# Copies of odd heads' v and the scaling of turned k moved from ScalarE to GpSimd, with a new list of the order of work

## The chip, the cores and the metric

The kernel runs on one core of a Trainium2 chip. The metric is the device time of one execution in microseconds, the median of several runs: 478.81 us for the kernel before (three runs, 478.62 to 479.23). One more execution was recorded by the profiler.

The engines are named as in the profile: PE is TensorE, ACT ScalarE, DVE VectorE, POOL GpSimd, SP SyncE, which here only issues DMAs.

## The reference

An attention block with a decaying state is followed by a feed-forward block of products. For each of 4 batches and 8 heads, over 768 steps t with head size 48:

```python
cur   = einsum('d,e->de', u * k[t], v[t])
y[t]  = einsum('d,de->e', r[t], state + cur)
state = w[:, None] * state + einsum('d,e->de', k[t], v[t])
```

y, laid out as 3,072 tokens of 384 numbers, goes through

```python
out = ((x @ w1) * (x @ w2)) @ w3 @ w_out
```

with w1 and w2 of 384 x 1024, w3 of 1024 x 1024 and w_out of 1024 x 384. The weights arrive as 64-bit numbers.

## The kernel before

**Tiling.** The sequence is cut into 6 chunks of 128 steps; a unit is one chunk of one batch, so there are 24 units, n = 4c + b. For each unit k and r are multiplied by powers of w (scale, L453), turned so that the head size lies on the partitions (on PE for units 0 to 4, turn_k L500; through DRAM for later ones), and k times r gives a masked 64 x 64 block for each half chunk and head. That block times v, plus r times the running state, is y. The term with u is made in two ways: for units 0 to 4 (EARLY, L447) the turned k is scaled by a column of u (put_u, L597, word ku) and multiplied with r on PE (own_products, L603, word Au), then laid on the diagonal of the masked block (own_mask, L607, word mo); for later units DVE multiplies k, r and u (L462, L465, L469) and ACT multiplies the sums with v (L483).

The products with odd heads read v from the other half of the partitions, so odd_values (L709, word vs) copies the odd heads' v of each unit crosswise, two copies of 64 x 192 per unit into one of three buffers. with_pairs (L725, word V) reads it.

**Weights.** Each weight comes in 32 pieces through three buffers (fetch, L266, word W; the first eight are strips of w1 and w2, the next eight are w_out, the last sixteen w3). A piece is converted in five words: M on ACT, N and H on DVE, L on ACT, Q on DVE; L frees the buffer. Then w3 and w_out are folded into one 1024 x 384 matrix: for each of eight blocks DVE turns a block of w3 (word G, L434), PE multiplies it with w_out (word F, L439), ACT takes it (word X, L442). From then on a chunk needs two products with w1 and w2 (words a and b, or in halves pa and pb with sums ga and gb) and one with the folded matrix (words P, each eight matmuls of 128 x 192, L829, with sums E, L845 to L859, and stores D, L863). The rows of the result are gathered in two buffers (`bufs=2`) taken in turn by the upper and lower rows of each pair.

**Order.** ORDER is a list of 1,417 words written out by hand or by a planner. A word names a step, its unit or piece, and the PSUM banks it takes. Each engine runs its instructions in the order of the list, and starts one when the semaphores of what it needs are there:

```python
with tc.manual_schedule(engines={PE, ACT, DVE, SP}):
    for word in ORDER.split():
        word, _, at = word.partition("/")
        chosen_banks[:] = map(int, at)
        name, *at = word.split(".")
        names[name](*map(int, at))
```

Of the words that the prediction speaks of, T, R, A, Au, S, U, V, yt, F and P are PE's; t, r, M, L, ku, vs, X and yx are ACT's; k, N, H, Q, i, j (state), m and mo (masks), fe, d, e, f, u, G and most of E are DVE's; v, kr, W, y, z and D are issued by SP. Z is a filler of matmuls whose result is not used (busy_array, L953). x, y, z and l turn k and r of later units through DRAM.

Of the kernel before, what the change touches and what calls it, by code (L numbers as in the profile page):

```python
# [27 lines left out]
fe.1/0 k.3 Au.2 V.1/10 L.2 W.4 i.2/4 R.3/2 m.2 kr.5 Y.1/10 T.3/4 r.3/2 k.4 yt.1/1 t.3/4 W.5 mo.2 ku.3 R.4/0 j.2/5  # L28
S.2/24 A.3 yx.1/1 Q.1 Au.3 yx.0/3 T.4/5 r.4/0 v.4 Q.2 a.0.0.0/1 M.3 N.3 vs.2 m.3 a.0.1.0/3 t.4/5 H.3 c.0.0.0/1 vs.3
N.4 U.3/05 L.3 fe.2/4 mo.3 V.2/24 c.0.1.0/3 i.3/0 M.4 k.5 A.4 v.5 Y.2/24 S.3/13 W.6 b.0.1.0/0 H.4 ku.4 fe.3/3 Q.3 L.4  # L30
yt.2/2 V.3/13 u.0.1.0/0 d.5 W.7 Au.4 Y.3/13 ub N.5 U.4/40 M.5 kr.6 yt.3/1 b.0.0.0/3 H.5 yx.3/1 yx.2/2 vs.4 Q.4
a.0.2.2/1 L.5 cz.1 N.6 vs.5 W.8 j.3/5 Q.5 a.0.0.1/2 kr.7 u.0.0.0/3 M.7 N.7 a.0.1.1/5 c.0.2.2/1 H.7 x.5 a.0.5.2/3 L.7
# [5 lines left out]
c.0.7.2/4 W.18 Q.15 M.17 N.17 Q.14 z.6 H.17 b.0.7.2/5 u.0.3.2/1 L.17 Q.17 W.20 G.0 b.0.6.2/4 M.18 cz.0 v.7 N.18 M.19
N.19 H.18 H.19 L.18 F.0/1 x.7 c.0.4.2/3 W.21 L.19 Q.18 Q.19 M.20 W.22 N.20 vs.6 e.6 H.20 G.1 L.20 W.23 f.6 M.21 F.1/3
Q.20 N.21 y.7 H.21 u.0.6.2/4 L.21 M.22 Q.21 W.24 G.2 N.22 H.22 F.2/4 j.5 L.22 N.23 M.23 W.25 u.0.4.2/0 yx.4/2 H.23  # L40
Q.22 L.23 l.6 Q.23 W.26 N.24 M.24 G.3 X.1/3 z.7 S.5/02 U.6 fe.5/2 H.24 M.25 A.6 d.7 V.5/02 L.24 kr.8 N.25 F.3/3 H.25
Q.24 L.25 Y.5/02 M.26 W.28 Q.25 N.26 H.26 G.4 L.26 W.29 m.6 F.4/0 X.3/3 i.6 l.7 W.27 u.0.7.2/5 X.0/1 j.6 X.2/4 M.28
# [5 lines left out]
f.9 xs.1.0 pa.1.1.0/1 xs.1.1 s.0.0.0 pa.1.0.4/5 xs.1.2 wa.3 pa.1.0.5/3 E.0.1.1/0 d.10 pa.1.0.1/2 i.9 ga.1.0.1/3 vs.10
wb.0 xs.1.3 yt.8/0 ga.1.0.3/45 pa.1.0.6/3 yx.8/0 k.10 pb.1.0.0/0 ga.1.0.2/3 wb.2 ga.1.0.5/2 pa.1.0.3/3 m.9 vs.9 e.10
x.10 pb.1.0.4/2 ga.1.0.7/3 k.11 y.10 gb.1.0.0/30 pa.1.0.7/5 j.9 pa.1.0.2/4 wb.1 wb.3 z.10 ga.1.0.4/5 pb.1.0.5/3 B.0  # L50
pb.1.0.1/0 gb.1.0.1/3 kr.13 ga.1.0.6/4 gb.1.0.3/42 pb.1.0.6/3 kr.12 gb.1.0.5/0 f.10 pb.1.0.7/2 gb.1.0.2/3 pb.1.0.3/3
pb.1.0.2/4 gb.1.0.7/3 gb.1.0.4/2 ga.1.1.0/31 g.9 d.11 pa.1.1.5/3 B.1 kr.14 pa.1.1.1/1 B.3 ga.1.1.1/3 l.10 x.11
# [1033 lines left out]
```

## Time and profile before

| | us |
|---|---|
| median of three runs | 478.81 |
| lowest and highest | 478.62, 479.23 |
| the profiled execution | 479.13 |
| its span | 477.0 |

| engine | busy us | share of the span |
|---|---|---|
| PE | 463.4 | 97% |
| DVE | 324.3 | 68% |
| ACT | 199.4 | 42% |
| POOL | 4.4 | 1% |

The span runs from the first instruction to the last event of the profiled execution; the 2.1 us between it and the execution's time lie around it. A matmul's end is modelled, so PE's busy share is a share of time in which it had work, not of its peak. In the rows below, an instruction's "idle before" is the time its engine stood still before it, followed by what released it.

### The profile page before, as it was taken

How to read it: one execution, taken by the hardware profiler on the slowest of the kernel's cores; microseconds unless marked ns; L12 is line 12 of the kernel's file. 1: busy time of each engine (PE TensorE's matmuls, PEld its weight loads, DVE VectorE, ACT ScalarE, POOL GpSimd, SP SyncE). 2: the span in 40 equal slices, each digit the busy share in tenths (PEclk: the TensorE clock that was granted, in tenths of full speed). 3: DMA queues.
4: the chain of work that ended last, by engine and by line, in shares of the span. 5: the costliest groups of instructions: out<-in, count | busy, mean ns of one | idle time of the engine just before them, and what ended most of it. 6: DMA issues, size and time to landing. Idle time of an engine off the chain costs nothing. (4 is left out here: it accounts for less than half of the span.)

```text
span 477.0 us, 12147 instructions
## 1 busy us (share of the span) xinstructions
PE 463.4 (97%) x5072; PEld 391.3 (82%) x5072; DVE 324.3 (68%) x668; ACT 199.4 (42%) x464; POOL 4.4 (1%) x17
## 2 busy tenths in 40 slices
...
GB/s 180 234 283 240 205 225 211 225 218 200 155 68 118 122 114 110 141 68 166 116 133 105 52 99 118 48 53 85 1 84 1 19 16 26 8 18 0 35 36 88
DMA packets 100481, 52.74 MB, mean 111 GB/s; under 512 B 79296, under 2 KB 89792, under 8 KB 100416
## 3 DMA queue, kind: packets, MB, share of 16 engines
...
q14 instruction: 23, 0.19, 0.1%
q10 hardware_dynamic: 624, 0.00, 0.1%
...
## 5 line engine op out<-in xcount | busy, mean ns | idle before, releaser
L917 PE MATMUL ps_accB<-x,w 128*128 128x256 f32 x160 | 45.1, 384 | 0.0
L439 PE MATMUL ps_w<-wo,w3T 128*128 128x384 f32 x128 | 42.5, 488 | 0.5 <-DVE w3T L434 0.3
L483 ACT ACTIVATE ynat<-vnat,dg 128x48 f32<-128x48 f32 x144 | 34.3, 323 | 17.8 <-DVE dg L469 14.7
L439 PEld LDWEIGHTS ps_w<-wo,w3T 128*128 128x128 f32 x128 | 24.0, 190 | 17.5 <-ACT t L420 0.9
L917 PEld LDWEIGHTS ps_accB<-x,w 128*128 128x128 f32 x160 | 29.3, 190 | 4.0 <-ACT u3a L934 0.4
L420 ACT ACTIVATE t<-raw 128x512 uint32<-128x512 uint32 (+2 forms) x32 | 22.6, 712 | 23.0 <-DVE w3n L416 16.3
L453 DVE TENSOR_TENSOR krs<-krin,pn_in 128x768 f32<-128x768 f32 x24 | 22.7, 950 | 2.3 <-ACT pn_in L336 2.0
L921 PE MATMUL ps_accB<-xT,w 128*128 128x256 f32 x80 | 23.8, 379 | 0.0
L921 PE MATMUL ps_accC<-xT,w 128*128 128x256 f32 x80 | 23.8, 379 | 0.0
L771 PE MATMUL ps_b<-xT,w 128*128 128x512 f32 (+1 forms) x60 | 22.3, 514 | 1.1 <-ACT ynat L736 1.1
L917 PE MATMUL ps_Ab<-xT,w 128*128 128x256 f32 x80 | 22.5, 383 | 0.0
L917 PE MATMUL ps_Aa<-xT,w 128*128 128x256 f32 x80 | 22.3, 381 | 0.0
L539 ACT COPY kT<-tt 128x1024 f32<-128x1024 f32 x19 | 19.9, 1046 | 4.0 <-PE ps_y L702 2.5
L771 PE MATMUL ps_a<-xT,w 128*128 128x512 f32 (+1 forms) x60 | 21.3, 507 | 0.0
L747 ACT COPY xT<-ps_x 128x384 f32<-128x384 f32 x24 | 11.2, 475 | 22.6 <-PE ps_x L741 22.5
L771 PEld LDWEIGHTS ps_b<-xT,w 128*128 128x128 f32 x60 | 11.0, 190 | 10.9 <-issue 7.8
L523 DVE STREAM_TRANSPOSE tr<-krs 128x768 f32<-128x768 f32 x19 | 18.4, 970 | 0.1
L633 DVE COPY_PREDICATED AT<-later,ps_a 128x512 f32<-128x512 int32 x24 | 17.5, 728 | 0.8 <-PE ps_a L582 0.4
L771 PEld LDWEIGHTS ps_a<-xT,w 128*128 128x128 f32 x60 | 11.3, 190 | 7.8 <-issue 6.7
L829 PE MATMUL ps_a11b<-w,abt 128*128 128x192 f32 x96 | 17.7, 327 | 0.0
L829 PE MATMUL ps_a22t<-t,abt 128*128 128x192 f32 x96 | 17.5, 327 | 0.0
L709 ACT COPY vodd<-vnat 64x192 f32<-64x192 f32 x48 | 16.8, 350 | 1.6 <-DMA vnat<-in_v_dram 0.6
...
## 6 DMA issues: line engine op xcount, KB each, us to landing
...
```

Of the source, the lines that this page charges most:

```text
L420: nc.scalar.activation(out=part["t", i], in_=words(i)[0], func=COPY, scale=2.0 ** -29)
L439: nc.tensor.matmul(ps, lhsT=w3T[j][:, kc].rearrange("x b k -> x (b k)"), rhs=wo[kc], start=(kc == 0), stop=(kc == KF - 1))
L453: nc.vector.tensor_mul(krs[n % NS][:, which, :, :D], kr[:, which], pn[:, which, :, :D])
L483: nc.scalar.activation(out=ynat[n][:, h, :], in_=vnat[n % NV][:, h, :], func=COPY, scale=dg[n][:, h:h + 1])
L523: nc.vector.transpose(out=blocks[n].rearrange("x m e t -> x e m t"), in_=krs[n % NS][:, :, :, :D])
L539: nc.scalar.copy(out=turned(n).rearrange("x g p (z t) -> x (g p) z t", t=Q), in_=tts.rearrange("x z e t -> x e z t"))
L633: nc.vector.copy_predicated(AT[n], later.bitcast(I32)[:, None, None, :].to_broadcast([C, 2, NP, T]), upper(n))
L709: nc.scalar.copy(out=vodd[n % NV][rows(a)], in_=vnat[n % NV].rearrange("t (p i) d -> t i p d", i=2)[rows(1 - a), 1])
L771: nc.tensor.matmul(ps, lhsT=(w1 if x == "a" else w2)[:, z, q, js], rhs=xT[c][:, q, ts], start=(q == 0), stop=(q == KM - 1))
L829: nc.tensor.matmul(ps, lhsT=operand(c, j // 2, a)[:, j % 2, m * C:(m + 1) * C], rhs=w34[:, KH * (x == 1) + j, :DH] if x < 2 else made[b][: ...
L917: nc.tensor.matmul(ps, lhsT=quarter(w, g, i, x), rhs=(b11, b21, b22, t4, b12, t2, t3)[x], start=x in (0, 4) and i == 0, stop=True, skip_gr ...
L921: nc.tensor.matmul(ps, lhsT=wide_of[w][:, g + half * HZ, 2, i * P:(i + 1) * P], rhs=xT[c][:, 2, side * TH:(side + 1) * TH], start=False, s ...
```

## The change

The two ScalarE operations become GpSimd operations, and GpSimd joins the engines whose order the list sets. Unit 0's k and r are scaled by two words, ka.0 and kb.0, in place of k.0. The filler Z, which stood at three places with 4 + 1 + 3 calls, stands at one with 4. Otherwise the new list has the words of the old one, in another order and with other banks. Of ORDER the beginning, the lines around piece 16 (W.16), those around block 6 of the fold (G.6) and the end are shown.

```diff
-PE, ACT, DVE, SP = (getattr(mybir.EngineType, x) for x in ("PE", "Activation", "DVE", "SP"))
+PE, ACT, DVE, SP, POOL = (getattr(mybir.EngineType, x) for x in ("PE", "Activation", "DVE", "SP", "Pool"))
...
 ORDER = """
-v.1 kr.2 W.2 vs.0 k.0 k.1 Z.4/1 T.0/0 R.0/1 t.0/0 U.0/23 r.0/1 N.0 M.0 i.0/2 A.0 W.1 uw j.0/3 U.1/45 v.2 ku.0 H.0
-R.1/0 kr.3 i.1/4 vs.1 Z.1/1 Au.0 j.1/5 L.0 T.1/1 k.2 t.1/1 m.0 r.1/0 Z.3/3 R.2/2 ku.1 T.2/3 mo.0 S.0/45 Q.0 A.1 M.2
-Au.1 N.2 t.2/3 fe.0/5 m.1 V.0/45 kr.4 M.1 S.1/10 N.1 mo.1 Y.0/45 r.2/2 H.1 yt.0/3 v.3 ku.2 U.2/45 H.2 A.2 W.3 L.1
...
-H.10 Q.6 L.10 b.0.1.1/3 W.13 Q.10 f.5 M.9 a.0.6.2/5 N.9 d.6 z.5 H.9 u.0.2.2/4 L.9 M.11 N.11 Q.9 W.12 a.0.7.2/4 H.11
-x.6 L.11 M.13 W.14 u.0.1.1/3 N.13 H.13 b.0.0.1/3 Q.11 L.13 y.6 j.4/0 l.5 W.16 m.4 b.0.5.2/0 c.0.3.2/1 mo.4 M.12 v.6
...
-G.6 yt.5/1 P.0.1.0/4 yx.5/1 X.4/0 N.27 H.27 F.6/1 i.7 L.27 k.9 M.31 W.30 g.6 Q.27 N.31 z.8 G.5 x.9 v.8 F.5/0 H.31 y.9
...
-E.4.1.3/3 E.4.0.7/1 s.5.1.2 D.4.0.1 P.4.1.4/0 P.5.0.0/3 E.4.1.5/4 E.4.1.6/4 E.4.0.4/2 E.4.1.4/0 P.5.1.5/1 D.4.1.0
-D.4.0.0 P.5.1.2/4 P.4.1.6/2 E.5.1.2/4 E.4.1.1/5 E.5.0.0/3 P.5.1.3/0 P.5.1.1/4 E.5.1.3/0 E.5.1.6/1 s.5.1.3 P.5.0.3/5
-P.5.1.6/3 P.5.0.5/0 E.5.1.7/3 E.5.1.1/4 E.4.1.7/2 D.5.1.1 D.4.1.1 P.5.0.2/3 P.5.0.4/4 E.5.0.2/3 E.5.0.3/5 P.5.0.1/2
-E.5.0.4/4 E.5.0.5/0 E.5.0.6/0 D.5.0.0 P.5.0.6/3 P.5.1.4/5 E.5.0.7/3 E.5.0.1/2 E.5.1.5/1 D.5.0.1 E.5.1.4/5 D.5.1.0
+v.1 kr.2 k.1 W.1 uw ka.0 T.1/2 kb.0 T.0/3 t.1/2 R.0/4 t.0/3 R.1/5 r.0/4 ku.0 U.0/01 A.0 N.0 M.0 Au.0 W.2 H.0 vs.1 kr.3
+i.0/0 vs.0 L.0 m.0 Z.4/4 S.0/23 ku.1 j.0/1 r.1/5 v.2 U.1/40 mo.0 fe.0/3 A.1 k.2 Au.1 Q.0 T.2/5 R.2/1 i.1/4 t.2/5 m.1
+V.0/23 M.1 ku.2 S.1/45 mo.1 kr.4 r.2/1 N.1 Y.0/23 A.2 fe.1/5 H.1 j.1/0 L.1 Au.2 W.3 V.1/45 m.2 Y.1/45 W.4 k.3 U.2/12
...
+y.5 mo.4 L.10 a.0.6.2/5 M.9 N.9 W.13 H.9 Q.10 L.9 M.11 N.11 W.12 H.11 b.0.5.2/3 u.0.2.2/1 L.11 c.0.6.2/5 Q.9 W.14 M.13
+k.6 N.13 b.0.6.2/2 z.5 H.13 Q.11 L.13 M.12 Q.13 W.16 N.12 H.12 a.0.1.1/1 x.6 L.12 M.14 W.15 N.14 c.0.3.2/0 u.0.5.2/3
...
+A.7 P.0.0.0/4 G.6 N.27 F.6/0 H.27 m.7 L.27 i.7 yx.4/3 W.30 Q.27 M.31 Y.6/15 z.8 G.5 k.9 v.8 F.5/3 N.31 H.31 x.9 M.30
...
+P.5.0.0/1 E.4.1.4/0 s.5.1.2 E.4.0.5/2 P.5.0.1/4 E.4.1.5/5 E.5.0.0/1 D.4.1.0 P.5.0.2/0 P.5.0.3/2 E.5.0.2/0 E.4.0.4/3
+E.5.0.1/4 D.4.0.0 P.5.0.6/1 E.5.0.3/2 P.5.0.4/0 P.5.0.5/3 P.5.1.2/4 E.5.0.6/3 E.5.0.5/3 E.5.0.7/1 E.5.0.4/0 D.5.0.1
+E.4.1.6/5 P.5.1.3/2 D.5.0.0 P.5.1.0/3 P.4.1.6/1 E.5.1.0/3 P.4.1.1/0 P.5.1.4/5 E.4.1.1/0 E.4.1.7/1 E.5.1.2/4 D.4.1.1
+E.5.1.3/2 P.5.1.5/3 P.5.1.1/0 E.5.1.5/3 E.5.1.4/5 D.5.1.0 P.5.1.6/1 E.5.1.1/0 E.5.1.6/3 E.5.1.7/1 D.5.1.1
 """
...
         def put_u(n):
             for p in range(NP):
-                nc.scalar.activation(out=kuT[:, p, :], in_=kT[n][:, p, :], func=COPY, scale=uw[:, p, :])
+                nc.gpsimd.tensor_scalar(kuT[:, p, :], kT[n][:, p, :], uw[:, p, :], None, ALU.mult)
...
             for a in range(2):
-                nc.scalar.copy(out=vodd[n % NV][rows(a)], in_=vnat[n % NV].rearrange("t (p i) d -> t i p d", i=2)[rows(1 - a), 1])
+                nc.gpsimd.tensor_copy(out=vodd[n % NV][rows(a)], in_=vnat[n % NV].rearrange("t (p i) d -> t i p d", i=2)[rows(1 - a), 1])
...
-            with tc.manual_schedule(engines={PE, ACT, DVE, SP}):
+            with tc.manual_schedule(engines={PE, ACT, DVE, SP, POOL}):
```

The words ka and kb are in the table of names of the kernel before: scale(n, slice(0, 1)) and scale(n, slice(1, 2)).

## Rows read from the trace of the kernel before

**Rows 1.** The page, busy us, share of the span and instructions.

```profile
PE 463.4 (97%) x5072; PEld 391.3 (82%) x5072; DVE 324.3 (68%) x668; ACT 199.4 (42%) x464; POOL 4.4 (1%) x17
```

**Rows 2.** Stretches: length, each engine's busy us, granted clock, DMA share, GB/s.

```profile
9.39:69.30 59.91, 56.05 (x964) 39.34 (x964) 52.77 (x98) 43.66 (x93) 0.00 (x0) 1.00 0.88 239
69.30:126.53 57.23, 55.84 (x486) 33.66 (x490) 54.32 (x95) 33.47 (x63) 0.00 (x0) 1.00 0.85 205
126.53:444.00 317.47, 317.47 (x3433) 285.24 (x3425) 200.15 (x412) 118.97 (x303) 0.00 (x0) 1.00 0.28 73
444.00:477.00 33.00, 27.24 (x168) 26.95 (x166) 12.80 (x33) 0.32 (x1) 0.00 (x0) 0.99 0.17 57
```

**Rows 3.** Time lines of DVE and PE at the fold's blocks 6 and 7.

```profile
113.26 1.25 DVE L434 STREAM_TRANSPOSE w3T<-w3n 128x1024 f32<-128x1024 f32 x1
...
115.05 10.48 PE L439 MATMUL ps_w<-wo,w3T 128*128 128x384 f32 x32
...
125.28 1.25 DVE L434 STREAM_TRANSPOSE w3T<-w3n 128x1024 f32<-128x1024 f32 x1
...
127.40 5.33 PE L439 MATMUL ps_w<-wo,w3T 128*128 128x384 f32 x16
```

**Rows 4.** DVE's waits, 9.39 to 69.3: us in total, times, longest.

```profile
DVE t L413 <- DMA raw<-in_moe_w_dram: 2.8, 3, 1.8
...
DVE t L413 <- DMA raw<-in_moe_w_out_dram: 0.8, 2, 0.6
```

**Rows 5.** Time lines of DVE and SP around words N.13, W.16 and N.16.

```profile
58.54 0.36 DVE L413 TENSOR_SCALAR t<-raw 128x384 uint32<-128x384 uint32 x1
...
63.30 1.83 SPq L266 DMA_DIRECT2D raw<-in_moe_w_dram  x4
...
69.30 0.43 DVE L413 TENSOR_SCALAR t<-raw 128x512 uint32<-128x512 uint32 x1 [1.80 <-DMA raw<-in_moe_w_dram]
```

**Rows 6.** Groups by line: ACT's copies and scalings; total us, mean ns, idle before.

```profile
L709 ACT COPY vodd<-vnat 64x192 f32<-64x192 f32 x48 | 16.8, 350 | 1.6 <-DMA vnat<-in_v_dram 0.6
...
L597 ACT ACTIVATE tt<-kT,uw 128x128 f32<-128x128 f32 x20 | 6.5, 412 | 0.0
```

**Rows 7.** Groups by line: POOL, all in the first 5.3 us.

```profile
L217 POOL MEMSET AT<- 128x512 f32 x2 | 1.0, 533 | 0.0
...
L198 POOL COPY later<-square 64x64 f32<-64x64 f32 x2 | 0.5, 232 | 0.1
...
L195 POOL TENSOR_SCALAR_AFFINE_SELECT square<-square 128x128 f32<-128x128 f32 x1 | 0.3, 292 | 0.0
```

**Rows 8.** Time lines of DVE and POOL, 2.5 to 5.5 us.

```profile
3.28 0.59 DVE L307 TENSOR_SCALAR wn_in<-wucol 128x4 f32<-128x4 f32 x1 [2.08 <-DMA wucol<-in_w_dram]
3.90 0.17 DVE L309 TENSOR_TENSOR wn_in<-wn_in 128x4 f32<-128x4 f32 x1
...
3.32 1.01 POOL L217 MEMSET AT<- 128x512 f32 x2
```

**Rows 9.** Groups by line: DVE's scaling and a multiplication of half its size.

```profile
L453 DVE TENSOR_TENSOR krs<-krin,pn_in 128x768 f32<-128x768 f32 x24 | 22.7, 950 | 2.3 <-ACT pn_in L336 2.0 <-PE ps_a L575 0.3
...
L462 DVE TENSOR_TENSOR ruk<-krin 128x384 f32<-128x384 f32 x19 | 10.4, 547 | 0.1
```

**Rows 10.** Time lines of PE, DVE and SP at the end.

```profile
465.88 1.46 PE L829 MATMUL ps_a22t<-t,abt 128*128 128x192 f32 x8
467.18 1.46 PE L829 MATMUL ps_a12b<-w,abt 128*128 128x192 f32 x8
...
469.78 1.46 PE L829 MATMUL ps_a22t<-t,abt 128*128 128x192 f32 x8
...
467.38 0.35 DVE L853 TENSOR_TENSOR osb_low<-u,ps_a22t 128x192 f32<-128x192 f32 x1 [0.49 <-PE ps_a22t L829]
...
472.00 0.36 DVE L855 TENSOR_TENSOR osb_low<-ps_s1t,u 128x192 f32<-128x192 f32 x1 [1.40 <-DMA out_dram<-osb_low]
472.27 0.34 DVE L853 TENSOR_TENSOR osb_low<-u,ps_a22t 128x192 f32<-128x192 f32 x1
...
468.03 0.33 SPq L863 DMA_DIRECT2D out_dram<-osb_low  x1
```

More of the change, by code (lines that the diff above doesn't have):

```diff
@@ L28 @@
[L28 to L32, printed above, removed]
@@ L38 @@
[L38 to L42, printed above, removed]
@@ L48 @@
[L48 to L52, printed above, removed]
@@ new lines @@
+gb.1.1.5/2 S.10/31 A.11 fe.10/1 B.3 V.10/31 l.12 pb.1.1.5/5 E.0.1.2/4 i.11 P.0.1.4/2 Y.10/31 gb.1.1.1/5 d.12 j.11
+P.0.1.3/4 kr.15 k.13 pa.1.1.2/0 E.0.1.3/4 s.1.0.0 e.12 m.11 pa.2.0.0/3 x.13 pb.1.1.6/5 f.12 S.11/14 gb.1.1.2/5 U.12
+fe.11/4 V.11/14 A.12 Y.11/14 v.14 pb.1.1.3/5 v.13 k.14 y.13 E.0.1.4/2 i.12 yt.11/1 d.13 pb.2.0.0/4 yx.11/1 j.12
+ga.1.1.6/0 vs.14 yt.10/2 gb.1.1.7/5 P.0.1.5/1 yx.10/2 vs.12 ga.2.0.0/53 xs.2.0 vs.13 xs.2.1 P.0.0.3/2 z.13 xs.2.2
+E.0.1.5/1 E.0.1.6/1 e.13 pa.2.0.5/5 E.0.0.3/2 D.0.1.0 x.14 pb.1.1.4/1 ga.2.0.1/5 f.13 P.0.0.4/2 y.14 xs.2.3 s.0.0.3
@@ new lines @@
+i.14 d.14 j.14 pb.2.0.4/1 kr.17 ga.2.0.6/0 s.1.0.2 yx.13/4 pb.2.0.3/5 l.15 v.15 gb.2.0.3/01 s.1.0.3 z.16 e.14
+pb.2.0.7/1 f.14 P.0.0.1/2 gb.2.0.7/5 g.14 gb.2.0.4/1 pb.2.0.2/0 s.1.1.0 vs.15 m.14 E.0.0.1/2 vs.16 pa.2.1.0/4 S.14/12
+ga.2.1.0/54 U.15 fe.14/2 E.0.0.7/3 A.15 s.1.1.1 V.14/12 d.16 pa.2.1.1/4 e.16 kr.19 gb.2.0.6/0 Y.14/12 pa.2.1.5/5 m.15
+ga.2.1.5/4 l.16 f.16 pa.2.1.4/3 k.17 ga.2.1.1/5 P.0.1.6/1 i.15 g.15 j.15 pa.2.1.6/5 d.18 S.15/24 ga.2.1.3/03
+ga.2.1.2/5 U.16 fe.15/4 A.16 k.18 V.15/24 pa.2.1.3/5 Y.15/24 v.18 v.17 E.0.1.7/1 e.18 f.18 pb.2.1.0/2 m.16 ga.2.1.7/5
```

141 lines of the change are left out of this document (73 added, 68 removed).

## The prediction

> **What bounds the kernel now.** I read the page first, then a table by stretches, then the waits and time lines of the stretches that were not full. On the page [rows 1] TensorE (PE) is busy 97% of the span: whatever ends the kernel passes through it. GpSimd (POOL) does nothing in any of the stretches read next. The stretches [rows 2] say where PE's missing time lies: 3.9 us of idle from 9.39 to 69.3, 1.4 from there to 126.53, none at all from 126.53 to 444, and 5.8 in the last 33 us. So the long middle can't be shortened by moving work between other engines; it can only begin earlier, and the tail behind the last product can get shorter. ScalarE (ACT), from which the change takes work, is busy 43.7 + 33.5 = 77.1 us of the 117.1 between 9.39 and 126.53, VectorE (DVE) 52.8 + 54.3 = 107.1: there DVE is the scarce engine.
>
> The hand-over from the DVE-fed start to the full middle is the fold, PE's words F.0 to F.7, each of which needs a turned block (word G) from DVE. G.6 starts at 113.26 and takes 1.25, F.6 starts at 115.05: 0.54 us to spare; G.7 ends at 126.53 and F.7 starts at 127.40: 0.87 [rows 3]. PE runs without a gap behind F.6, so the end moves with F.6, and F.6 can't move more than half a microsecond unless G.6 does. Both lists have the same PE words ahead of F.6 and F.7, but for four warm-up calls.
>
> Of DVE's 7.1 us of idle up to 69.3 half is for weights on their way: 2.8 us for w1, w2 and w3 and 0.8 for w_out [rows 4]. The longest is one wait of 1.80 us in front of N.16, the first piece of w3, whose loads SP issued only at 63.30, behind y.6 [rows 5].
>
> **What leaves ACT.** 48 copies of 0.350 us and 20 scalings of 0.412 us, 16.8 + 6.5 us of busy time [rows 6]. Ahead of G.7 these are 18 copies and 20 scalings. ACT is not what DVE or PE mostly waits for there, so I give this nothing by itself; what it buys is a list in which conversions are not queued behind copies.
>
> **What they cost on POOL.** No row shows these two operations there. The nearest are a copy of 64x64 at 0.232 us, a select over 128x128 at 0.292, and a memset of 512 elements at 0.533 [rows 7]. For the copy of 64x192 the ends are 0.23 and 0.53; I take 0.34, about the short copy plus 128 elements at the slope between the first two, 0.9 ns. For the scaling of 128x128 I take the select's 0.29. The 38 instructions ahead of G.7 then hold POOL 18 x 0.34 + 20 x 0.29 = 11.9 us of 117: no bound. POOL's order puts vs.1 and vs.0 behind ku.0, and ku.1 behind them; a scaling waits for the turned k of its unit and for the u-term's products of the unit before, and PE's Au word and DVE's mo word wait for it. Four scalings in a row are 1.17 us, against 1.29 on ACT: no loss, if DVE leaves POOL alone.
>
> **Does it?** At 3.28 us a TENSOR_SCALAR of four elements on DVE took 0.59 us; it ended with POOL's first memset of AT, which started at 3.32 and took 0.53 [rows 7]. The next DVE operation on the same four elements, a TENSOR_TENSOR, took 0.17 under POOL's second memset [rows 8]. So one kind of DVE instruction is held until a POOL instruction ends and one kind is not, at least against a POOL instruction that reads nothing. No row has a DVE operation on two SBUF tensors beside a POOL instruction that reads SBUF, which is what the new copies are. Bounds: 0, or every POOL instruction adds its whole length to a DVE instruction of the held kinds. Those (N, H, Q, k, d, e and half of j) are about two thirds of DVE's time, so the upper end is 0.67 x 11.9 = 8.0 us ahead of G.7; a gain is excluded, since DVE itself loses no work. I take 0.8: in the first 36 us most copies and scalings fall beside PSUM-fed words or DVE waits, vs.4 and vs.5 fall into the wait for N.16, and three units' copies (six of 0.34) remain, at some 40% of their length.
>
> The Trainium skill ("SBUF — State Buffer", section "SBUF: two separate sides") states a lock here: DVE instructions in a two-port mode, or with two SBUF inputs against a GpSimd instruction that reads SBUF, share one pair of ports with GpSimd, and whoever comes second is blocked for the whole instruction. The first half agrees with the 0.59 us above; the second half no run here shows yet. By it the sum would be 483.8, the third rival below.
>
> **Unit 0's k and r in two instructions.** k.0 of 0.95 us becomes ka.0 and kb.0 of about 0.55 each, by the 128x384 multiplication's 0.547 [rows 9]: +0.15 us of DVE. In the new list they stand behind k.1 and uw, so unit 0 starts about 1 us later than now; nothing that ends late hangs on it, as F.6 lies 100 us on.
>
> **The new list, up to the fold.** I price each DVE word by the mean of its group and add in list order. Up to G.7 that is 117.8 us now and 118.5 in the new list (+0.15 for ka and kb, +0.55 for e.7, which moves ahead); the union of the busy time now is 107.1, as neighbours overlap: a factor of 0.91. So DVE can't finish G.7 earlier by doing less. It can by waiting less. Now N.13 starts at 58.54 and W.16's four loads at 63.30 [rows 5]. In the new list 0.8 us less stands ahead of N.13, so it starts at about 57.8; L.13 frees the buffer for W.16 at about 59.6; y.6 is no longer ahead of W.16 on SP, and z.5 behind W.14 fits in before. W.16 is issued at 59.6 instead of 63.3 and lands 3.7 us earlier: N.16 at 65.6. By the same sum DVE is ready for N.16 at about 64 to 65, so it waits about a microsecond. From N.16 to G.6 the new list has 2.3 us more in it than the old, x 0.91 = 2.1. G.6 therefore comes 3.7 - 2.1 - 0.8 = 0.8 us earlier, and PE, which has more room before it than now, gives up 0.4 of the 0.54: **F.6 moves by -1.2 us.** The four warm-up calls that go were idle-time filler; the granted clock is 1.00, the 2.4 GHz level, in every stretch up to 444 [rows 2], and PE would stand still some 1.8 us before its first transposes. I count nothing for it.
>
> SP issues the same DMAs in another order, so nothing is added there.
>
> **The tail.** Now PE's last product starts at 469.78. The same subtraction one product row earlier began 1.50 us behind its product (465.88 to 467.38). The last one begins at 472.27, 2.49 behind, because the DVE word ahead of it waited 1.40 us for a store to give its row buffer back (SP issued it at 468.03) [rows 10]. In the new list the last words are P.5.1.6 and E.5.1.7. Their row buffer is that of D.4.1.1, which is issued 3.0 us ahead of the last product's start (P.4.1.1 starts 4 x 1.30 = 5.2 before; E.4.1.1 and E.4.1.7 follow 1.5 behind it) and, at 3.97 as now, lands 0.9 behind it. E.5.1.1 and E.5.1.6 then take 0.27 + 0.27 and E.5.1.7 goes at 1.50, as PE allows. It fits with nothing to spare: **-1.0 us**, or -0.6 if that store takes 0.4 longer.
>
> **The sum.** The profiled execution took 479.13 us with a span of 477.0. 479.13 - 1.2 - 1.0 = 476.9; the median of the three runs, 478.81, lies 0.3 below the profiled one, so I forecast 476.6.
>
> **Rivals.**
> - *Only the tail* (0.18). Loads, not SP's order, set N.16: the DMA share is 0.88 up to 69.3 and 0.85 after [rows 2]. G.6 stays, F.6 gains up to 0.4: 477.4 to 477.8. At the slow end with the store late: 478.2.
> - *DVE stops waiting altogether* (0.14). Some 5 of its 7.1 us of idle up to 69.3 go, and POOL takes nothing back: G.6 moves by -5 + 0.6 (the 0.7 us of added words, x 0.91) = -4.4, and with the tail 473.4 comes out; with a little left over, 474.
> - *POOL holds DVE up* (0.18). At the upper end of the bound DVE loses 8.0 us ahead of G.6 in place of 0.8: F.6 moves by -1.2 + 7.2 = +6.0, with the tail's -1.0: 483.8. Half of it gives 480.2. For it: the row at 3.28. Against it: PSUM-fed words between. It decides once the 38 instructions cost DVE more than 0.8 + 1.2 + 1.0 = 3.0 us, 79 ns each.
> - *The list does not carry* (0.08). Behind 126.53 PE has no idle now, so any new order there can only be as good or worse; a word of POOL or DVE late by a microsecond or two: 478 to 480.
>
> **How the numbers follow.** The forecast's case, 475 to 477.8, has 0.42. A measurement of this kernel can tell about 0.2%, 0.96 us: faster is below 477.85, slower above 479.77. Faster: 0.40 + 0.14 and a third of the first rival, less some doubt on the tail's exact fit: 0.57. Slower: 0.16 of the held-up DVE, 0.03 of the last rival and 0.05 of what I don't see: 0.24. The rest, 0.19, is the same. The range leaves out the best of the second rival and the worst of the third: 473.8 to 481.0.
>
> **What would show it.** Right: W.16's loads issued near 60 and N.16 near 66; F.6 near 114; PE full from there; the last product followed 1.5 us later by its sum; POOL's copies near 0.34 us, DVE's groups at their present means. Wrong: N, H, Q and k longer than now by tenths of a microsecond beside POOL rows, PE idle behind 126.53, or DVE waiting for POOL's kuT in the first 36 us.

## The result, and the profile of the kernel after

The changed kernel takes 486.51 us, median of 4 runs (486.10 to 486.81), beside 479.02 for the kernel before in the same set of runs: a ratio of 1.0144, 95% interval 1.0105 to 1.0182. It is 1.4% slower, outside the predicted range; the forecast, 476.6, had the wrong sign.

The profiled execution took 486.75 us with a span of 485.0, so 8.0 us more span than before. The page of the changed kernel, engines and two groups of POOL:

```profile
span 485.0 us, 12190 instructions
PE 466.0 (96%) x5064; PEld 393.4 (81%) x5064; DVE 326.3 (67%) x669; ACT 175.7 (36%) x396; POOL 43.2 (9%) x85
...
L709 POOL COPY vodd<-vnat 64x192 f32<-64x192 f32 x48 | 20.8, 434 | 299.9 <-DMA vnat<-in_v_dram 297.8
L597 POOL TENSOR_SCALAR tt<-kT,uw 128x128 f32<-128x128 f32 x20 | 18.1, 917 | 13.1 <-ACT kT L507 11.0 <-PE ps_y L725 1.9
```

ACT's sum fell by 23.7 us, the two groups that it was to lose [rows 1, 6], and DVE's grew by only 2.0. What stands out is the second group: a scaling costs 0.917 us on POOL in the mean, three times what the prediction took. The mean hides two things. The first two lines give duration in ns as lowest, median and highest; the others are single instructions:

```profile
L597 POOL TENSOR_SCALAR tt<-kT,uw x20: 597/604/2446, 12.5 to 38.9; 128x128 f32<-128x128 f32 x20
L709 POOL COPY vodd<-vnat x48: 339/343/785, 15.7 to 356.7; 64x192 f32<-64x192 f32 x48
...
30.63 0.95 DVE L423 CUSTOM_DVE_ANT_0 w<-w,t 128x1536 uint16<-128x1536 uint16 x1
30.71 2.45 POOL L597 TENSOR_SCALAR tt<-kT,uw 128x128 f32<-128x128 f32 x1
31.50 0.96 DVE L416 SCALAR_TENSOR_TENSOR w<-w,t 128x768 uint32<-128x768 uint32 x1
33.14 0.60 POOL L597 TENSOR_SCALAR tt<-kT,uw 128x128 f32<-128x128 f32 x1
```

Eleven of the twenty scalings take 0.60 us, twice the 0.29 that was forecast. The other nine take 0.72 to 2.45. The longest, at 30.71, began 0.08 us after the start of a DVE instruction with its inputs in SBUF and lasted until 0.7 us behind the second of two such instructions. Spans on POOL are rough, but the starts say the same: the four scalings from 30.14 on begin 0.58, 2.43 and 0.58 us apart. This is a pattern: four profiles have all twenty scalings on POOL (this one, e2, e5 and e7 below). Of 27 scalings begun while DVE ran an instruction on SBUF alone, 26 took longer than 0.65 us; of the 53 others 2 did, though in 23 of these such an instruction began while the scaling ran. So DVE, when it is first, holds POOL up. At 0.60 each the twenty would be 12.1 us instead of 18.3, so about 6.3 us of the group are such delays. The copies' median is 0.343 us, the price that was forecast; their mean, 0.434, has such delays in it too.

A table by stretches, cut at the same events as [rows 2] (start of N.16, end of G.7), says where time went:

```profile
9.39:75.01 65.62, 57.20 (x926) 39.81 (x926) 51.99 (x94) 34.22 (x62) 22.99 (x32) 0.97 0.77 210
75.01:134.36 59.35, 57.37 (x543) 35.13 (x543) 56.15 (x102) 31.07 (x58) 3.45 (x6) 1.00 0.87 211
134.36:451.00 316.64, 316.64 (x3395) 284.70 (x3394) 201.61 (x413) 106.81 (x270) 12.44 (x30) 1.00 0.28 73
451.00:485.00 34.00, 27.45 (x167) 27.00 (x165) 12.29 (x32) 0.64 (x2) 0.00 (x0) 0.95 0.15 50
```

The first stretch is 5.7 us longer than before (65.62 for 59.91), with PE's idle up from 3.9 to 8.4; the second is 2.1 longer; in the third PE is full as before. DVE's busy time in the first stretch is lower than before (51.99 for 52.77), so it is not slower work that makes DVE late there: it waits. The waits (total us, times, longest), first DVE's from 9.39 to the start of N.13 at 66.66, then PE's up to 76 us:

```profile
DVE AT L633 <- PE ps_a L603: 5.3, 4, 1.9
DVE krs L453 <- ACT pn_in L336: 2.0, 1, 2.0
DVE w L416 <- ACT w L408: 1.8, 1, 1.8
DVE half L621 <- PE ps_u L575: 1.4, 1, 1.4
...
PE ps_a L603 <- POOL tt L597: 4.1, 9, 1.0
PE ps_kT L500 <- DVE uw L593: 1.9, 1, 1.9
```

This is a chain of three engines. PE's Au word (L603) waits for POOL's scaling; DVE's mask m (L633) stands in its queue waiting for PE to get through Au; and behind the mask stand the conversions of the weights. All rows of DVE's waits up to N.13 add up to 12.7 us, in the kernel before, up to its N.13 at 58.54, to 5.0: 7.7 more, and N.13 is 8.1 later. From there the lateness runs on as the prediction described it, with the sign turned. The lines of DVE, SP and PE:

```profile
66.66 0.36 DVE L413 TENSOR_SCALAR t<-raw 128x384 uint32<-128x384 uint32 x1
70.27 1.78 SPq L266 DMA_DIRECT2D raw<-in_moe_w_dram  x4
75.01 0.43 DVE L413 TENSOR_SCALAR t<-raw 128x512 uint32<-128x512 uint32 x1 [1.37 <-DMA raw<-in_moe_w_dram]
120.63 1.25 DVE L434 STREAM_TRANSPOSE w3T<-w3n 128x1024 f32<-128x1024 f32 x1
122.02 10.56 PE L439 MATMUL ps_w<-wo,w3T 128*128 128x384 f32 x32
134.50 5.40 PE L439 MATMUL ps_w<-wo,w3T 128*128 128x384 f32 x16
```

W.16's loads go out at 70.27 (63.30 before [rows 5]), N.16 starts at 75.01 (69.30), F.6 at 122.02 (115.05 [rows 3]): 7.0 late. POOL's own time line shows the scalings of units 0 to 4:

```profile
12.54 3.06 POOL L597 TENSOR_SCALAR tt<-kT,uw 128x128 f32<-128x128 f32 x4 [7.37 <-ACT kT L507]
17.29 4.01 POOL L597 TENSOR_SCALAR tt<-kT,uw 128x128 f32<-128x128 f32 x4
23.14 3.32 POOL L597 TENSOR_SCALAR tt<-kT,uw 128x128 f32<-128x128 f32 x4 [1.85 <-PE ps_y L725]
30.14 4.18 POOL L597 TENSOR_SCALAR tt<-kT,uw 128x128 f32<-128x128 f32 x4 [3.67 <-ACT kT L507]
36.02 3.48 POOL L597 TENSOR_SCALAR tt<-kT,uw 128x128 f32<-128x128 f32 x4
```

Four in a row take 3.06 to 4.18 us where ACT took 1.29: 2.4 by themselves, and 0.7 to 1.8 beside DVE's instructions. The tail, and below it the last store of the kernel before:

```profile
476.99 1.46 PE L829 MATMUL ps_s4b<-w,raw 128*128 128x192 f32 x8
478.49 0.36 DVE L859 TENSOR_TENSOR osb_top<-ps_s4b,u 128x192 f32<-128x192 f32 x1 [0.68 <-PE ps_s4b L829]
478.88 0.33 SPq L863 DMA_DIRECT2D out_dram<-osb_top  x1
```

```profile
472.65 0.33 SPq L863 DMA_DIRECT2D out_dram<-osb_low  x1
```

The last sum begins 1.50 us behind the last product, as predicted (2.49 before [rows 10]), and the last store is issued 1.89 behind it in place of 2.87. But the span ends 6.1 us behind that store's issue in place of 4.3. So the sum against before is: F.7 +7.1; from F.7 to the last product 342.49 for 342.38, +0.1; the tail -1.0; behind the last store +1.8: 8.0 of span. Around the span 1.75 us lie in place of 2.13, which leaves 7.6 for the profiled executions.

### The profile page after: what moved, and what is told of

Same layout as the page of the kernel before. It is cut to its first block, busy times and chain, and to the rows that moved or that the text cites. A ratio compares the mean times of both kernels' runs of the same rounds, so it can differ in the third digit from the quotient of the medians.

```text
span 485.0 us, 12190 instructions
## 1 busy us (share of the span) xinstructions
PE 466.0 (96%) x5064; PEld 393.4 (81%) x5064; DVE 326.3 (67%) x669; ACT 175.7 (36%) x396; POOL 43.2 (9%) x85
## 4 chain that ended last, share of the span: by engine, by line
PE 82%; DVE 4%; SPq 3%; POOL 3%; DMA 3%; issue 2%; ACT 2%; ACTq 0%; DVEq 0%; POOLq 0%
PE ps_accB L917 11%; PE ps_w L439 7%; PE ps_accC L917 4%; PE ps_Ab L917 4%; PE ps_Aa L917 4%; PE ps_accB L921 4%; PE ps_accC L921 4%; PE ps_s1t L829 3%; PE ps_a11b L829 3%; PE ps_s4b L829 3%; PE ps_s2t L829 3%; PE ps_a12b L829 3%; PE ps_a22t L829 3%; PE ps_s3t L829 3%; POOL tt L597 3%; SPq L266 2%
## 5 line engine op out<-in xcount | busy, mean ns | idle before, releaser
L709 POOL COPY vodd<-vnat 64x192 f32<-64x192 f32 x48 | 20.8, 434 | 299.9 <-DMA vnat<-in_v_dram 297.8
L453 DVE TENSOR_TENSOR krs<-krin,pn_in 128x768 f32<-128x768 f32 (+1 forms) x25 | 22.9, 919 | 2.7 <-ACT pn_in L336 2.0
L771 PE MATMUL ps_a<-xT,w 128*128 128x512 f32 (+1 forms) x60 | 23.4, 539 | 0.0
L633 DVE COPY_PREDICATED AT<-later,ps_a 128x512 f32<-128x512 int32 x24 | 17.6, 732 | 5.4 <-PE ps_a L603 5.3
L597 POOL TENSOR_SCALAR tt<-kT,uw 128x128 f32<-128x128 f32 x20 | 18.1, 917 | 13.1 <-ACT kT L507 11.0
L582 PE MATMUL ps_a<-kT 64*64 64x64 f32 x768 | 17.0, 221 | 2.2 <-issue 0.8
L771 PEld LDWEIGHTS ps_a<-xT,w 128*128 128x128 f32 x60 | 12.3, 209 | 8.4 <-issue 7.2
```

The lines of the kernel that those rows point to most:

```text
L453: nc.vector.tensor_mul(krs[n % NS][:, which, :, :D], kr[:, which], pn[:, which, :, :D])
L597: nc.gpsimd.tensor_scalar(kuT[:, p, :], kT[n][:, p, :], uw[:, p, :], None, ALU.mult)
L709: nc.gpsimd.tensor_copy(out=vodd[n % NV][rows(a)], in_=vnat[n % NV].rearrange("t (p i) d -> t i p d", i=2)[rows(1 - a), 1])
L771: nc.tensor.matmul(ps, lhsT=(w1 if x == "a" else w2)[:, z, q, js], rhs=xT[c][:, q, ts], start=(q == 0), stop=(q == KM - 1))
```

## The experiments

Two theories at first. **Latency**: the scalings' price on POOL sits in every unit's chain. **Lock**: POOL's instructions, whichever they are, hold DVE up (the prediction's third rival; the scalings held up by DVE, above, are the other direction and part of the latency). A third possibility is that the new **list** is slower by itself. All runs in one table; "list" is the old or the new one, "u" and "v" say where scalings and copies run. F.6 is its start; "middle" is the last product's start less F.7's; "store" is the last store's issue behind the last product; "end" is the span behind that issue, all of the profiled execution. Ratios stand against the kernel before on the same chip, whose median was 479.0 to 480.5. e11, e13, e14 and e17 scale only one of a unit's four blocks: the u-term of three quarters of the heads is left out in units 0 to 4, so they show times and not a usable kernel.

| run | list, u, v | ratio, 95% | F.6 | middle | store | end |
|---|---|---|---|---|---|---|
| before | old, ACT, ACT | | 115.05 | 342.4 | 2.9 | 4.3 |
| after | new, POOL, POOL | 1.0144, 1.0105 to 1.0182 | 122.02 | 342.5 | 1.9 | 6.1 |
| e1 | new, ACT, POOL | 1.0076, 1.0050 to 1.0102 | 117.46 | 342.8 | 1.9 | 6.4 |
| e2 | new, POOL, ACT | 1.0133, 1.0116 to 1.0150 | 122.80 | 344.7 | 2.1 | 5.3 |
| e3 | new, ACT, ACT | 1.0161, 1.0116 to 1.0207 | 120.70 | 344.8 | 1.9 | 5.0 |
| e4 | old, ACT, POOL | 1.0061, 1.0044 to 1.0078 | 115.15 | 344.8 | 3.1 | 6.4 |
| e5 | old, POOL, ACT | 1.0095, 1.0063 to 1.0127 | 119.54 | 342.4 | 3.1 | 4.4 |
| e6 | new, POOL in one, POOL | 1.0115, 1.0085 to 1.0145 | 119.00 | 342.5 | 1.9 | 6.2 |
| e7 | after and calls | 1.0153, 1.0121 to 1.0184 | 121.51 | 342.6 | 1.9 | 6.2 |
| e8 | before and free tile | 0.9987, 0.9970 to 1.0005 | 115.93 | 342.4 | 1.9 | 4.3 |
| e9 | old, POOL in one, ACT | 1.0011, 0.9988 to 1.0033 | 116.97 | 342.4 | 3.0 | 4.4 |
| e10 | e9 and free tile | 0.9989, 0.9974 to 1.0003 | 115.73 | 342.4 | 1.9 | 4.3 |
| e11 | new, a quarter on POOL, POOL | 1.0091, 1.0057 to 1.0125 | 117.36 | 342.9 | 1.9 | 6.1 |
| e12 | before and four DMAs | 1.0035, 1.0013 to 1.0056 | 116.01 | 342.4 | 3.2 | 6.4 |
| e13 | e11 and calls, badly placed | 1.0213, 1.0161 to 1.0265 | 125.18 | 343.6 | 1.9 | 6.4 |
| e14 | e11 once more | 1.0060, 1.0033 to 1.0086 | 121.06 | 342.5 | 1.9 | 6.3 |
| e15 | before once more | 0.9993, 0.9974 to 1.0012 | 115.23 | 342.4 | 2.5 | 4.4 |
| e16 | e8 once more | 0.9981, 0.9958 to 1.0003 | 115.27 | 342.4 | 1.9 | 4.7 |
| e17 | e11 and calls | 1.0117, 1.0087 to 1.0148 | 120.35 | 342.9 | 1.9 | 6.4 |
| e18 | before without calls | 1.0001, 0.9983 to 1.0020 | 114.81 | 342.4 | 3.2 | 4.4 |

F.6 is one execution's number: the old start with ACT's scalings gave 114.81 to 116.01 over seven profiles, e11's kernel 117.36 and 121.06. A difference in F.6 between two single profiles, in the new list above all, is uncertain by microseconds; the ratios carry the verdicts.

### Undoing one half, or doing one half alone: e1 to e5

e1 and e2 put one group of the changed kernel back on ACT, e3 both; e4 and e5 move one group in the kernel before.

```diff
# e1, e3: in put_u          (e5: the other way round, in before)
-                nc.gpsimd.tensor_scalar(kuT[:, p, :], kT[n][:, p, :], uw[:, p, :], None, ALU.mult)
+                nc.scalar.activation(out=kuT[:, p, :], in_=kT[n][:, p, :], func=COPY, scale=uw[:, p, :])
# e2, e3: in odd_values     (e4: the other way round, in before)
-                nc.gpsimd.tensor_copy(out=vodd[n % NV][rows(a)], ...
+                nc.scalar.copy(out=vodd[n % NV][rows(a)], ...
```

> The changed kernel with the 20 scalings of turned k back on ScalarE and everything else as changed. Theory 'latency' (each unit's four scalings took 3.1 to 4.2 us on GpSimd in place of 1.29 on ScalarE, and TensorE's Au word and the masks behind it wait for them): the 7 us go, F.6 near 115 or before, 476.5 to 479.5 us. Rival 'lock' (GpSimd's instructions hold VectorE up, whichever they are): 20 of the 68 are gone, part of the loss stays, 480.5 to 484 us. Rival 'list' (the new order itself is worse): 484 to 487 us.

> The changed kernel with the 48 copies of v back on ScalarE, the scalings still on GpSimd. Latency: the scalings stay slow, 485 to 488 us. Lock: the 48 copies are most of GpSimd's time, so 480.5 to 484 us. List: 484 to 487 us.

> The changed kernel with both groups back on ScalarE: the new list and the two-part scaling of unit 0 alone. Latency: 477 to 480 us (ScalarE has the copies to do again, in a list that was made without them). Lock: the same, 477 to 480 us, since nothing is left on GpSimd. List: 484 to 487 us.

> The kernel before with its old list, only the 48 copies of v on GpSimd. Latency: nothing waits for these copies closely, 478 to 479.5 us. Lock: 18 copies ahead of the fold of up to 0.43 us each on VectorE, 481 to 485 us.

> The kernel before with its old list, only the 20 scalings of turned k on GpSimd. If the scaling's latency is what costs (four in a row took 3.1 to 4.2 us on GpSimd, 1.29 on ScalarE, and five units go through it ahead of 45 us), F.6 moves from 115.05 to 117 or later and the time is 482 to 487 us on this chip, whose time before is 480.5. If the old list has slack there and only the new list is tight, F.6 stays within 0.5 us and the time is 480 to 481.5.

None of the three fits all five. Read F.6 and the middle apart. At F.6, the scalings on POOL cost 4.6 us in the new list (after less e1) and 4.5 in the old one (e5 less before): latency, in the size expected. In time it is 0.7% (1.0144 for 1.0076), about 3 us, in the new list (the two intervals just fail to touch) and 0.95%, 4.5 us, in the old one. The copies on POOL cost nothing there (e4: 115.15 for 115.05), so POOL holding DVE up is not it; e4's time, 483.51, lies in that theory's range, but it is lost in the middle and at the end. But e1 keeps 2.4 us, so the new list's start is slower by itself; that part of the latency theory falls. The two moves do not simply add up in the new list: with the copies on ACT, the scalings on POOL make F.6 2.1 us later (e2 less e3) and the time no longer (1.0133 for 1.0161). In the middle there is a rule nobody had put forward: with its copies on the engine that the list was made with, either list needs 342.4 to 342.9 us (343.6 in e13, where PE waits 0.9 us for DVE); on the other engine (e2, e3 new; e4 old) 344.7 to 344.8. In e3, PE's waits behind 133 us are for ACT, which has the copies to do again:

```profile
PE ps_accB L917 <- ACT u3b L934: 1.5, 1, 1.5
```

Two more, of 0.4 and 0.3, bring them to 2.2 of the 2.4 us. In e4 one sees DVE and POOL lengthen each other's work. The lines of DVE and POOL near 138 us in e4, and below them the same DVE word in the kernel before:

```profile
137.80 2.15 POOL L709 COPY vodd<-vnat 64x192 f32<-64x192 f32 x4 [12.33 <-DMA vnat<-in_v_dram]
138.92 0.83 DVE L811 TENSOR_TENSOR s<-abt,abt 128x512 f32<-128x512 f32 x1
```

```profile
138.79 0.68 DVE L811 TENSOR_TENSOR s<-abt,abt 128x512 f32<-128x512 f32 x1
```

A subtraction with both inputs in SBUF takes 0.15 us longer beside the copies, and the four copies 2.15 in place of 1.53 (the row of four at 15.66 us in the changed kernel). The Trainium skill ("SBUF — State Buffer", section "SBUF: two separate sides") states this lock. The traces agree that it exists, in both directions: the scaling at 30.71 above was held for 1.85 us, and e9 below has DVE held for 0.84. DVE's sum is small here: its groups add up to 326.3 us in the changed kernel and 324.8 in e3, which has neither group on POOL, so 1.5 us over 68 POOL instructions, 22 ns each. Of the 2.4 us that e4 lost in the middle, 0.7 is a wait of PE for DVE at 452 us; the rest comes in pieces that I did not follow.

### The scaling's price: e6 and e9

```diff
-            for p in range(NP):
-                nc.gpsimd.tensor_scalar(kuT[:, p, :], kT[n][:, p, :], uw[:, p, :], None, ALU.mult)
+            nc.gpsimd.tensor_tensor(out=kuT, in0=kT[n], in1=uw.to_broadcast([P, NP, C]), op=ALU.mult)
```

e6 is the changed kernel with this, e9 the kernel before with it (in place of ACT's four).

> The changed kernel with a unit's four scalings on GpSimd as one multiplication of 128x512 by the broadcast column. If a GpSimd instruction costs mostly a fixed price, one of them takes 1.0 to 1.8 us in place of 3.1 to 4.2 for four, TensorE's waits for it go, and F.6 comes from 122.0 to 116.5 to 118.5: 481 to 484 us. If it goes by elements, it takes 3 us or more, F.6 stays near 122, and the time 486 to 488.5.

> The kernel before with its old list; a unit's four scalings become one multiplication of 128x512 on GpSimd (1.04 us in the run that had it, 1.29 for four on ScalarE). If ScalarE's load sets the pace of the first 40 us, the 6.5 us taken from it bring F.6 from 115.05 to 113 to 114.5 and the time to 0.5 to 2 us below before. If the chain of a unit sets it, the gain per unit is at most 0.25 us and the hand-over takes it back: the time within 0.5 us of before, or above it.

The first group lines of e6 on POOL:

```profile
L596 POOL TENSOR_TENSOR tt<-kT,uw 128x512 f32<-128x512 f32 x5 | 5.2, 1039 | 17.6 <-ACT kT L507 17.5
```

One instruction over 512 elements takes 1.04 us, four undisturbed ones over 128 each 2.4 (0.60 each in the changed kernel, 0.606 in e11's group below): less than half. The two are different operations, so this does not split the 0.60 into a fixed part and one that goes by elements. F.6 came down by 3.0 us, not quite to e1's level; in time the gain is not clear of noise (1.0115, its interval overlaps that of the changed kernel). The Trainium skill ("GPSIMD Engine Reference", section "Elementwise — side-by-side cycle accounting") gives 1.03 cycles of a 1.2 GHz clock per element for a short body: an estimate from it is 0.11 us for the 128 elements, and the 0.61 measured is mostly something else. For two inputs its 2.6 cycles per element make an estimate of 1.1 us for 512; the trace agrees with 1.04.

In e9 the lighter ACT gains nothing: 1.0011, and F.6 no earlier. That fits the expectation's second reading, by which a unit's chain sets the start, but does not show it, since DVE lost time as well. Two instructions of DVE and one of POOL in e9, and below them the same two of DVE in the kernel before:

```profile
28.45 2.66 DVE L423 CUSTOM_DVE_ANT_0 w<-w,t 128x1536 uint16<-128x1536 uint16 x2
28.73 1.57 POOL L596 TENSOR_TENSOR tt<-kT,uw 128x512 f32<-128x512 f32 x1 [7.83 <-ACT kT L507]
```

```profile
27.42 1.82 DVE L423 CUSTOM_DVE_ANT_0 w<-w,t 128x1536 uint16<-128x1536 uint16 x2
```

The multiplication was held for 0.53 us by the first of the two, and the second was held by it: 0.84 us together. DVE's groups add up to 326.6 us in e9 for 324.3 before, 2.3 us for five multiplications, and to 328.4 in e6 for 324.8 in e3. So this form, with two inputs on POOL, costs DVE far more than the 22 ns above.

### The list at the price that was forecast: e11, e14

```diff
-            for p in range(NP):
+            for p in range(1):
                 nc.gpsimd.tensor_scalar(kuT[:, p, :], ...
```

> The changed kernel with only the first of a unit's four scalings (the u-term of three quarters of the heads is left out), so that a unit's scaling costs GpSimd some 0.8 us, less than the 1.17 us that the prediction counted for four. If the price of the scaling alone was wrong, the list does what the prediction said: W.16's loads near 60, F.6 near 114, 477 to 478.5 us. If the list's start is slow by itself, F.6 stays at 117 or later and the time at 481 to 485 us.

> e11 once more, beside the run with the calls and beside the kernel before on one chip. F.6 between 116.5 and 118.5, 483 to 485 us; N.16's wait for its loads and the 2.1 us of words between N.16 and G.6 as in e11.

POOL's group, DVE's waits from 9.39 to N.13 (61.62), N.13 and N.16, and the fold's lines in e11:

```profile
L597 POOL TENSOR_SCALAR tt<-kT,uw 128x128 f32<-128x128 f32 x5 | 3.0, 606 | 19.6 <-ACT kT L507 19.5
...
DVE krs L453 <- ACT pn_in L336: 2.0, 1, 2.0
DVE w L416 <- ACT w L408: 1.6, 1, 1.6
DVE AT L633 <- PE ps_a L603: 1.4, 1, 1.4
DVE AT L714 <- PE ps_y L702: 1.3, 2, 0.9
...
61.62 0.35 DVE L413 TENSOR_SCALAR t<-raw 128x384 uint32<-128x384 uint32 x1
69.91 0.43 DVE L413 TENSOR_SCALAR t<-raw 128x512 uint32<-128x512 uint32 x1 [1.34 <-DMA raw<-in_moe_w_dram]
115.97 1.25 DVE L434 STREAM_TRANSPOSE w3T<-w3n 128x1024 f32<-128x1024 f32 x1
117.36 10.56 PE L439 MATMUL ps_w<-wo,w3T 128*128 128x384 f32 x32
```

With the scaling at half of what I had counted, N.13 is still at 61.62, not at the forecast 57.8: with three waits that are not shown (1.1, 0.3 and 0.3) DVE waits 8.0 us up to there, 5.0 before. Those 3.0 us are N.13's lateness of 3.1. Behind N.13 the prediction holds in kind: from N.16 (69.91) to G.6 are 46.06 us, before 43.96, so 2.10 more where 2.1 was counted. Over the ten profiles of this list it is 1.7 to 2.2 more in five, 2.9 to 3.0 in three and 4.3 in two; the next section says why. F.6 follows G.6's end by 0.14 in place of 0.54, the 0.4 that PE was to give up. e14 missed its expectation, with F.6 at 121.06 and 4.3 more from N.16 to G.6. The price was wrong, but it was not the only thing.

### Order or clock? e7, e13, e17, e18

The granted clock was 1.00, the 2.4 GHz level, in every stretch up to 444 us of the first profile of before [rows 2]. In the changed kernel it is 0.53 from 34.27 to 37.68 us, mostly the 1.2 GHz level, and e14's worse profile has several such stretches: 0.81 on average from 9.39 to 23.7 and 0.59 from 71.4 to 79. Stretches at 0.50 stand ahead of F.6 in all ten profiles of the new list, and in three of ten of the old one (e8, e9, e15). The same code up to the tail ran once with a stretch and once without, in e9 and in e10; the rows from 22 to 27 us:

```profile
22.00:27.00 5.00, 3.98 (x131) 3.76 (x132) 4.58 (x8) 2.31 (x4) 0.00 (x0) 0.68 0.83 179
```

```profile
22.00:27.00 5.00, 4.28 (x142) 3.51 (x141) 4.91 (x9) 3.53 (x8) 0.02 (x1) 1.00 0.93 208
```

F.6 came at 116.97 with it and 115.73 without: 1.2 us, one pair. From N.16 to G.6 the new list shows it better, since its ten profiles have the same words there. Five have no stretch at 0.50 there (the changed kernel, e1, e3, e11, e17), and the part is 1.7 to 2.2 us longer than the 43.96 of before; with 3.4 us at 0.50 (e6, e7, e13) it is 2.9 to 3.0 longer, with 6.8 us (e2, e14) 4.3. So 3.4 us at half clock cost about 1.0 us there and 6.8 about 2.4. e11 has 3.4 us at half clock up to F.6 and e14 13.7, and e14's F.6 is 3.7 us later. In the old list it can be less: e15 has such a stretch from 22.2 and its F.6, 115.23, is inside the range of those without. So warm-up calls were put into PE's idle (words `Z`), or taken out:

```diff
# e7, in after's list          # e13, e17: in e11's list        # e18, in before's list
-A.2 fe.1/5                    -uw ka.0 T.1/2                    -Z.4/1 T.0/0
+A.2 Z.4/1 fe.1/5              +uw ka.0 Z.8/1 T.1/2              +T.0/0
-A.3 M.3                       -r.0/4 ku.0     # e13             -Z.1/1
+A.3 Z.4/5 M.3                 +r.0/4 Z.4/5 ku.0                 -Z.3/3
                               -S.0/23 ku.1    # e17
                               +S.0/23 Z.8/4 ku.1
```

> The changed kernel with eight warm-up calls of TensorE put into its waits for GpSimd's scalings of units 2 and 3. If the stretch at the half clock (34.3 to 37.7 us) is owed to the idle ahead of it, the granted clock there goes to 1.00 and F.6 comes 0.5 to 1.7 us earlier; 485 to 486.5 us against 487.5 to 488 for the changed kernel on this chip. If the clock has no part in the loss, F.6 stays at 122 or comes later by the calls' own time, some 0.8 us.

> The changed kernel with one scaling of four, as in e11, and twelve warm-up calls more in TensorE's idle near 10.5 and 12 us. In e11 TensorE was busy 1.17 us of the 3.5 ahead of 19.3 and the granted clock was 0.55 in the 3.4 us that followed. If that stretch is a good part of the list's slow start, it goes with the calls, and F.6 comes from 117.4 to 115.5 to 116.5, 1 to 1.5 us below e14. If the list's order of waits sets it, F.6 stays within 0.5 us of that of e14, wherever the stretch lies.

> e14 with sixteen warm-up calls in TensorE's idle of the first 20 us, in banks that nothing holds (in e13 the calls stood 3.6 us in a bank that ScalarE had still to read, so it tells nothing). If the half-clock stretches behind that idle are the list's slow start, the executions' mean granted clock rises from 0.991 towards the 0.997 of before, F.6 comes to 115 to 116.5, and the time to 481 to 482 us (the end's 1.8 us stay). If the order sets it, the clock may rise, but F.6 stays at 117 or later and the time at 482.5 to 484.

> The kernel before without its three groups of warm-up calls (eight calls) in the unit stage. If they hold the clock, half-clock stretches come up in the first 40 us, each worth about 1.2 us by e9 against e10: mean granted clock 0.990 to 0.994, 1 to 3 us slower. If they only fill idle, the time is that of before within 0.5 us.

In e7 the clock is 1.00 from 34.27 to 37.68, but 0.50 in two other stretches (from 21.5 and from 76.1), and F.6 is 0.5 us earlier: inconclusive. In e13 the calls were badly placed: they waited 3.6 us for a bank that ACT had still to read, its ratio is 1.0213, and it says nothing about the clock. e17's mean granted clock over its executions is 0.993, e14's 0.990, before's 0.997; its F.6 is 120.35 and its time is above e14's. e18 lost nothing without its calls. So in the new list a stretch costs about a microsecond, but raising the mean a little did not bring the list's 2.4 us back. How large the clock's share is no run shows. For a large one: e11's one stretch, at 1.0 to 1.2 us, would be about half of its 2.3, and e14's seven executions go from 481.30 us at a mean clock of 0.993 to 485.97 at 0.984. Against it: one execution of e17 at 0.998 still took 484.67. What did show in e17 is idle of PE for which the profile has no releaser (waits of PE from 22 to 30 us):

```profile
PE ps_u L575 <- issue: 3.1, 1, 3.1
PE ps_y L702 <- issue: 1.3, 1, 1.3
```

How the list's 2.4 us divide between the order of its waits, the clock and such gaps stays open.

### The end: e12, and e8, e10, e15, e16

```diff
# e12, in sum_of_weights (four words near 150 us)
+            nc.sync.dma_start(out=outs[0:1, x:x + 1], in_=u[0:1, x:x + 1])
# e8, e10, e16, in rows_of_out
+                if (nm, c, m) == ("low", 5, 1):
+                    made[nm, c, m] = krin[0][:, 0].rearrange("t h d -> t (h d)")
```

> The kernel before with four DMAs of four bytes on SyncE near 150 us, which nothing waits for: SyncE runs at least 426 instructions in place of 422, as in the changed kernel. If the longer end behind the last store (6.16 us in the changed kernel, 4.31 before) comes from where SyncE's last instructions lie in its program, the span ends 5 to 6.4 us behind the last store's issue, and the time is 1 to 2 us above before. If it comes from the work on GpSimd, the end stays 4.3 us and the time is that of before within 0.5 us.

> The kernel before with one edit at the end: the last row buffer is a tile that is free by then, so the last sum waits for no store. The last sum begins 1.50 us behind the last product in place of 2.49; 1.0 us faster, 479.4 to 479.6 on this chip. If the end hangs on what SyncE does after the last store, nothing is gained: 480.3 to 481.

> The same with the free tile as last row buffer, too, which by itself brought the last store's issue from 1.73 to 0.74 us behind TensorE's last product: 0.6 to 1.0 us below the run with the one multiplication alone; faster than both kernels if that one is not slower than before.

> The kernel before, profiled once more on this chip, so that the runs beside it have a trace of the same chip. F.6 between 114.8 and 116.2 (115.05 in the first profile, 116.01 in the run with four DMAs, whose start is the same), the end 4.3 us behind the last store's issue, ratio 1.000.

> e8 once more, the kernel before with the free tile as last row buffer: 0.6 to 1.0 us below before. Together with e8 that should tell it from no change; if it comes out at or above before, the store's wait at the end is hidden by something else.

The instructions of the kernel's last line on SP (duration in ns; first and last start in us): before, after, e12.

```profile
L1081 SPq EVENT_SEMAPHORE  x10: 17/28/28, 475.6 to 476.9; - x10
```

```profile
L1081 SPq EVENT_SEMAPHORE  x10: 17/28/28, 481.9 to 485.0; - x10
```

```profile
L1082 SPq EVENT_SEMAPHORE  x10: 17/28/28, 477.2 to 480.4; - x10
```

Ten instructions of at most 28 ns take 1.3 us before, 3.1 after, and 3.2 in e12, where POOL does nothing but SP has four DMAs more, long over by then. So work on POOL is not needed for the longer end, nor does it bring it by itself: e5, e9 and e10 have the scalings on POOL and an end of 4.3 to 4.4. What e12 and the changed kernel have in common is a longer program of SP (422 instructions on record before, 426 in both), and one gap of 1.4 to 1.9 us opens inside that last row of waits, in all ten profiles with 426 to 430. In e2 and e3 (420) it is 0.6 to 0.9, so the number alone does not set it; in seven profiles with 422 there is none, in an eighth (e16) 0.3. That SP waits there for its own instructions is my reading of it; the trace shows the gap and not its cause. In time e12's four idle DMAs cost 0.35% (0.13 to 0.56).

The free tile does what it should: the store goes out 1.9 us behind the last product in place of 2.5 to 3.2. In time e8, e16 and e10 give 0.9987, 0.9981 and 0.9989, all below one and each interval just reaching over it: probably 0.1 to 0.2% faster than the kernel before, not shown by any of them alone. No other version came out below it.

## Why the prediction was wrong

- **"Four scalings in a row are 1.17 us, against 1.29 on ACT: no loss" is the step that failed most.** They took 3.06 to 4.18. The price came from a row of another kind [rows 7]: the select's 0.29 us stood for a scaling of 0.60, so four take 2.4 undisturbed. The other 0.7 to 1.8 us of a row of four came beside DVE's instructions. "If DVE leaves POOL alone" names that condition, but the working behind it prices only POOL holding DVE up and leaves the reverse at nothing. Price of the move: 4.5 us in F.6, one profile each, in either list (after less e1, e5 less before); in time 0.7 and 0.95%. No run divides it between the 0.60 and the delays.
- **"In the new list 0.8 us less stands ahead of N.13, so it starts at about 57.8" failed too.** That added up the words in DVE's queue and kept the old list's waits. Even with a scaling of 0.6 us N.13 stands at 61.62, and DVE waits 3.0 us more up to there, mostly for PE and ACT (e11); how much of this the order makes and how much the clock is open. "Unit 0 starts about 1 us later; nothing that ends late hangs on it" is the same error: DVE's conversions stand in the same queue behind that unit's masks.
- Right: the added words from N.16 to G.6 (2.1 us counted; 1.7 to 2.2 in the five profiles with the clock at 1.00 there), the 0.4 that PE gave up, PE full behind the fold.
- Right in size: DVE's loss by the port, 0.8 us for 38 instructions, 21 ns each; 22 measured over all 68. The third rival, which needed 79 ns, named a time nearer to the real one, 483.8, for the wrong reason: the two engines do hold each other up, but here it was POOL that lost, about 6.3 us of scalings.
- Right: the copies' 0.34 us (median 0.343; 0.434 in the mean, with the delays beside DVE); nothing ahead of the fold waited for them (e4's F.6).
- Right in the trace, lost in time: the tail's 1.0 us. It came, and 1.8 us behind the last store took it back. The prediction had nothing on that end.
- The warm-up calls counted as nothing: in the old list that holds (e18). That the clock would fall for a stretch or more in every profile of the new list was not foreseen.
- The fourth rival, that the list would not carry behind the fold, fell: 342.5 us for 342.4.
